# An order table redrawn, work for the tensor engine in early waits, and routing cut into pieces

## The chip, the core and the metric

The kernel runs on one core of a Trainium2 chip. The core has a tensor engine (TensorE, PE in the profile; its weight loads are shown apart as PEld), a vector engine (VectorE, DVE), a scalar engine (ScalarE, ACT), a general engine (GpSimd, POOL) and SyncE (SP), which here only issues transfers. Each runs its own queue in order; they meet at semaphores. The metric is device time in microseconds (us), and the time before is the median of three runs.

## What is computed

Attention first: for each of 8 batches and 8 heads, 512 tokens read from 32 states and the states read from the tokens. Both results together are 4,352 rows of 512 numbers. Then a mixture of 8 experts with soft routing: gate logits, a matrix P balanced by eight rounds of row and column normalization, and every expert applied to every row, weighted by P.

```
scores  = scale * x @ state.T          # softmax over states -> a
xread   = a @ state
scores2 = scale * state @ x.T          # softmax over tokens -> a2
sread   = a2 @ x
x = concat([xread, sread]) as (N, 512), N = 8 * (512 + 32)
P = exp(x @ w_gate - max)
for _ in range(8):
    P /= P.sum(1) + 1e-9
    P /= P.sum(0) + 1e-9;  P *= N / E
out = sum over e of P[:, e] * (relu(x @ w1[e]) @ w2[e])
```

(The reference here computes on N = 4,608 rows in the expert part's own set-up, but the kernel's rows are the 4,352 that attention gives.)

## The kernel before

Rows are handled in nine blocks: eight of 512 token rows (one per batch) and one of 256 state rows. The kernel has two stages.

The first stage does the attention, expert 0, the routing and the start of expert 1. It is a list of small operations (`op`), each with the engines it may run on, and `PLAN` is a table in the file that gives the order and the engine of each: `435P` is operation 435 on TensorE, V is VectorE, A ScalarE, G GpSimd, S a transfer from SyncE, H a step on the host side that only allocates. `issue` walks through the table and emits each operation; so the table sets the order of every engine's queue. An eviction (a copy out of PSUM) can be on ScalarE or on VectorE, as the table says.

Attention works in 16 units, two per batch (pairs of heads). For one unit: `turnX` (L578, by TensorE, batches 0 and 1) or a transposing transfer (L591, from SyncE, batches 2 to 7) turns x into `xT`; `score` (L605) makes scores in PSUM; the token side goes `flip` (L628), `maxA` (L631), `subA` (L648), `expA` (L656), `sumA` (L666), `normA` (L670), `flipA` (L674) and gives `aT`; the state side goes `maxB` (L640), `biasB` (L644), `expB` (L652), `recB` (L659), `normB` (L662), a transposing transfer to `ETs` (L742), and `read` (L758) with `keepS` into `xsT`. The first two units make the token side by matmul (`scoreA` L684, `turnA` L709) without the flips. Loads of x (L468) and of the weights w1 and w2 (L545, L548) are issued from GpSimd's queue; x has four buffers.

Expert 0 does not use the token rows themselves: w1 is projected through the states into V (L870), the hidden layer is V times `aT` (L897, eight per block), and the second product with w2 comes in half rows (L935, two halves for each 128 rows). The gate works likewise through a small product G (L520). The table mixes all this with attention, and then with the routing (part K, L814 to L846): a maximum, an exponential, and eight rounds of `rownorm` on VectorE (five instructions), a column sum by TensorE (L846) and `colnorm` (three instructions).

The second stage runs experts 1 to 7 in an order written out by hand: `layer1` makes the hidden layer of the next block (L255) while `layer2` does the seven Strassen-like products of this one (L334) and accumulates into `acc` (L348). Two PSUM banks (`seeds`) hold a running product; each was opened by a matmul with the identity (L353), and they are also used by `project` (L235), the projection for later blocks. `weigh` multiplies expert 0's result by its column of P (L296). `layer2_last` does the last block of the last expert: two rows of 128, and the transfers of the state rows to the output (L317).

Of the kernel before, what the change touches and what calls it, by code (L numbers as in the profile page):

```python
# [9 lines left out]
FP32 = mybir.dt.float32  # L10
# [7 lines left out]
46V 62P 50H 51G 61A 71V 63P 60A 52G 64V 11G 72V 73A 80P 65V 12G 435P 401P 66A 81V 13H 79P 14G 82V 436A 88V  # L18
437A 404P 83A 67V 402A 137H 403A 89V 96H 97P 100P 84V 406A 68V 90A 98A 15G 85V 69P 86P 53G 405A 99V 87V 70A
103P 101A 102A 91V 409P 16H 92G 413P 104V 407P 410A 411P 105V 111A 438P 120P 414V 408A 419P 421P 106V 415P  # L20
112V 138S 121V 74V 439A 412A 422V 113V 417P 107A 54G 440A 75G 122V 432P 429P 123V 370V 420A 469P 128A 418A
416A 17G 108V 140P 124A 125V 423P 426P 471A 433P 114A 148V 93S 129V 430P 149V 172H 424P 76S 434A 115V 470A
109G 130V 139S 110V 126G 141V 131A 427P 18G 127V 142V 428V 431A 445P 143V 132V 94P 150A 95V 77P 425A 156P 116G
447P 151V 133V 78V 449P 446A 443P 441P 144A 455P 164V 152G 448A 117S 19H 450V 157V 444A 165V 173S 442A 451P
456A 166A 134S 20G 452A 453P 463P 158V 472P 207H 145V 175P 159V 183V 184V 457P 31G 146G 454A 176V 473A 160A
464P 185A 174S 460P 458P 461P 465A 147V 161V 21G 153S 177V 191P 47P 162G 474A 118P 167V 459A 154P 462A 178V
163V 135P 49A 168G 199V 22H 48V 179A 466P 136A 352P 475P 200V 192V 201A 193V 119V 467P 476A 194V 23G 195A 485P
202V 208S 210P 180V 169S 155A 218V 356P 353A 481P 357V 468A 487P 219V 24G 489P 181G 186V 211V 242H 486A 482A
477P 490V 488A 483P 479P 220A 170P 478A 503P 187G 480A 484V 171A 203G 196V 537P 209S 25H 212V 226P 197G 504A
505A 506P 213V 500P 182V 198V 26G 234V 221V 507A 222V 204S 188S 491P 27G 538A 227V 539A 501P 497P 502A 508A  # L30
492P 235V 243S 228V 244S 214A 229V 511P 215V 236A 523P 230A 498P 494P 216G 245P 495P 515P 512V 499A 277H 231V
524A 493A 517P 246V 253V 223S 496A 247V 521P 516A 237V 254V 519P 509P 522V 518A 248V 513P 232G 189P 520A 255A
205P 510V 224P 514V 540P 28H 278S 261P 249A 190V 269V 29G 225A 270V 262V 531P 534P 206V 238G 250V 532P 256V
358P 271A 535P 217V 541A 533A 233V 542A 312H 279S 263V 272V 536A 354P 280P 528P 543P 529P 525P 288V 289V 251G
555P 264V 281V 265A 282V 239S 257V 526P 359A 266V 544A 530V 556A 545P 355A 547P 549P 273G 553P 527A 546V 571P
313S 290A 548A 283V 605P 550A 554V 296P 267G 606V 304V 572A 305V 240P 573A 557P 284A 607A 558A 551P 297V 552A
568P 360P 258S 241V 285V 30G 291V 306A 559P 562P 574P 298V 252V 315P 299V 286V 569P 576A 268V 323V 563P 575A
274S 300A 560P 570A 292G 316V 361A 561A 581P 564A 307V 565P 362P 324V 317V 301V 325A 302G 566P 363V 582A 326V
579P 587P 583P 287V 314S 588V 591P 567A 580A 639P 608P 584A 592A 347H 303V 331P 577P 348G 641V 640A 610A 609A
339V 293S 589P 585P 275P 332V 259P 578A 327G 586A 260A 590A 294P 340V 308G 333V 341A 593P 309S 318V 319A 334V  # L40
295V 364P 594P 276V 328S 625P 619P 342V 595A 335A 365A 599P 320V 602P 343V 336V 600P 337V 603P 626A 321G 322V
329P 310P 350G 344S 601A 349G 311A 620V 345P 338V 346V 604V 366P 596P 330A 368P 369V 351G 597P 367A 371V 611P
372P 598A 695H 615P 617P 373V 612V 374P 375V 613P 614V 616A 623P 618A 621P 696H 711H 376A 705P 377V 642P 624A
622A 706A 707A 630P 643V 697V 708P 644A 378P 379V 631P 710A 627P 698V 380V 647P 632A 709A 636P 628P 381P 633P
699V 648V 637P 382V 634P 657P 629A 638A 383V 700V 653P 658A 655P 384P 651P 635A 701V 654A 725P 385V 723P 386V
702V 656A 726A 716P 652A 724A 717A 645P 659P 649P 714P 646A 650A 660A 387P 721P 715A 712P 727P 687P 722A 388V
728A 688A 667P 713A 664P 389V 390P 703V 665P 668P 391V 673P 674A 392V 661P 670P 669A 729V 393P 671P 394V 666A
662P 672A 677P 395V 718P 663A 678A 679P 675P 683P 719A 681P 720V 680A 676A 685P 396P 684A 682A 397V 686A 692P
704V 689P 693P 690P 730P 398V 694A 399P 733P 731V 691A 732A 735A 734A 400V
""".split()  # L50
ENGINES = {"P": "PE", "V": "DVE", "A": "ACT", "G": "POOL", "D": "DMA", "S": "SPQ", "H": "HOST"}
NT_ = 2
# [52 lines left out]
def issue(ops):  # L105
    for step in PLAN:
        op = ops[int(step[:-1])]
        assert all(d.end for d in op.after) and ENGINES[step[-1]] in op.on
        for slot in op.takes:
            slot.ring.taken.append(slot)  # L110
            slot.tile = slot.make()
        op.emit(ENGINES[step[-1]])
        op.end = True
    assert all(op.end for op in ops) and len(PLAN) == len(ops)
# [3 lines left out]
def kernel(  # L118
# [63 lines left out]
    outs = out.rearrange("(b s) d -> b s d", s=SB)[:, S:, :]  # L182
# [80 lines left out]
    def layer1(e, bi):  # L263
# [6 lines left out]
        for j in range(NJ):  # L270
            for i in range(2):
                fb = i * NJ + j
                hps = bank([128, S], FP32, "hps", "h")
# [25 lines left out]
    def layer2_last():  # L299
# [4 lines left out]
        nb = 128 // Ns  # L304
        for row in range(tn // 128):
# [10 lines left out]
            for i in range(nb):  # L316
                (nc.scalar if i % 2 else nc.sync).dma_start(  # L317
                    out=outs[row * nb + i], in_=acc[ds(i * Ns, Ns), k, :])

    def layer2(e, bi, n):  # L320
# [30 lines left out]
        def seed(i):  # L351
            bb = bank([128, 2, DH], FP32, "Bseed", "B%d" % i)
            nc.tensor.matmul(bb.rearrange("p c d -> p (c d)"), identh, aT[:, 0, 0], start=True, stop=True)  # L353
            seeds.append(bb)

        if not n:
            for k, eng in enumerate(("DVE", "ACT", "DVE", "POOL")):
                weigh(k, eng)
        product(A, h(0, 0), w2h[:, :NJ, :DH], True)
        if not n:  # L360
            seed(0)
        Bb = seeds[n % 2]
        nc.scalar.copy(out=Bb[:, :nk], in_=A[:, :nk])  # L363
        yield
        product(Eb, s(0), T[:, 0], True)
        if not n:
            seed(1)
# [199 lines left out]
    for b in range(B):  # L567
# [30 lines left out]
        for q in range(NQ):  # L598
# [62 lines left out]
            def normB(eng, E2=E2, rrec=rrec):  # L661
                engines[eng].tensor_scalar(out=E2.tile, in0=E2.tile, scalar1=rrec.tile, scalar2=None,  # L662
                                           op0=ALU.mult)
# [33 lines left out]
            else:  # L697
                m0 = op(r(2), {"DVE": (0.63, 0.72)}, flip, [o2], [eA], [ps])
                m1 = op(r(3), {"DVE": (0.59, 0.68)}, maxA, [m0], [mxA], [eA])
                s1 = op(r(4), {"DVE": (0.60, 0.80)}, subA, [m1], [], [eA, mxA])  # L700
# [22 lines left out]
            n2 = op(r(3), {"DVE": (0.10, 0.25)}, biasB, [m2], [nsB], [nmB])  # L723
# [5 lines left out]
            f2 = op(r(6), {"DVE": (0.16, 0.26)}, recB, [e2], [rrec], [rowsum])  # L729
            f2 = op(r(6), {"DVE": (0.35, 0.48), "POOL": (1.56, 1.70)} if POOLB else {"DVE": (0.35, 0.48)}, normB, [f2], [], [E2, rrec])  # L730
# [33 lines left out]
            def keepS(eng, b=b, q=q, su=su):  # L764
                copy(eng, xsT[:, ds(2 * q, 2), ds(b * Ns, Ns)], su.tile)
# [38 lines left out]
    def sk(on, emit, after, **how):  # L804
        return op(rank, on, lambda _: emit(), after, **how)
# [6 lines left out]
    op((30.0,), {"DVE": (0.2, 0.3)}, lambda _: nc.vector.memset(ones128, 1.0))  # L812
# [8 lines left out]
    c = sk({"PE": (0.18, 0.45)}, lambda: nc.tensor.matmul(gb.tile, ones128[0:1, :], sm_["gm"]), [c], takes=[gb])  # L821
# [4 lines left out]
    for it in range(8):  # L826
        def rownorm():
            rsum = tile_of("rsum", [128, NTB])
            nc.vector.reduce_sum(out=rsum, in_=Pmat, axis=AX_X)
            nc.vector.tensor_scalar(out=rsum, in0=rsum, scalar1=EPS, scalar2=None, op0=ALU.add)  # L830
            nc.vector.reciprocal(out=rsum, in_=rsum)
            nc.vector.tensor_mul(Pmat, Pmat, rsum.unsqueeze(2).broadcast_to((128, NTB, E)))
            nc.vector.reduce_sum(out=tile_of("cpart", [128, E]), in_=Pmat.transpose([0, 2, 1]), axis=AX_X)

        csb = psum([128, E], FP32, "csb_ps")

        def colnorm(csb=csb):
            crec = tile_of("crec", [128, E])
            nc.vector.tensor_scalar(out=crec, in0=csb.tile, scalar1=EPS, scalar2=None, op0=ALU.add)
            nc.vector.reciprocal(out=crec, in_=crec)  # L840
            nc.vector.scalar_tensor_tensor(out=Pmat, in0=crec.unsqueeze(1).broadcast_to((128, NTB, E)),
                                           scalar=float(N) / float(E), in1=Pmat,
                                           op0=ALU.mult, op1=ALU.mult)

        c = sk({"DVE": (2.10, 2.25)}, rownorm, [c])
        c = sk({"PE": (0.25, 0.60)}, lambda csb=csb: nc.tensor.matmul(csb.tile, ones128, sm_["cpart"]),  # L846
               [c], takes=[csb])
        c = sk({"DVE": (0.75, 0.90)}, colnorm, [c], uses=[csb])
# [193 lines left out]
    for i, (e, bi) in enumerate(work):  # L1042
# [11 lines left out]
        if i:  # L1054
            next(v, None)
# [54 lines left out]
```

## Time and profile before

| | us |
|---|---|
| median of three runs | 753.16 |
| runs | 753.22, 753.16, 752.12 |
| the profiled execution | 752.75 |
| its span | 751.0 |
| PE busy from 0 to 10, from 10 to 20 | 3.15, 7.86 |
| PE busy from 50 to 60, from 60 to 70 | 8.99, 9.55 |
| PE busy from 200 to 300 | 100.00 |
| GpSimd busy from 11 to 101 | 43.90 |

The profile is of one execution. Busy times are those of each engine; matmuls are pipelined and their ends are modelled, so a full TensorE in this table need not be one at its peak. The granted clock is the share of TensorE's full clock that its throttle gave. A chain of waits follows the work that ended last back from the end, at each step to what released it.

### The profile page before, as it was taken

Reading aid. Unit: us, or ns where it says so; the run is one execution under the profiler, and the core shown is the slowest. Engines: PE = TensorE matmul, PEld = TensorE weight load, DVE = VectorE, ACT = ScalarE, POOL = GpSimd, SP = SyncE. Lnnn points to the kernel's source line nnn. Section 1 sums busy time; section 2 is a strip of 40 time slices with the busy share of each in tenths; the row PEclk is TensorE's granted clock in tenths of the full one; section 3 lists DMA queues with packets and bytes.
Section 4 is the critical chain, followed back from the end, with each engine's and each line's share of the span. In section 5 each row is a group of like instructions: output and inputs, shape, how many; then the busy total and the mean of one; then the engine's idle time right before and its main releaser. Section 6 shows DMA issues by size and latency. Waiting matters only on the chain.

```text
span 751.0 us, 16151 instructions
## 1 busy us (share of the span) xinstructions
PE 736.0 (98%) x6517; PEld 502.2 (67%) x6517; DVE 617.0 (82%) x1529; ACT 517.7 (69%) x1014; POOL 70.8 (9%) x81
## 2 busy tenths in 40 slices
PE   5999999999999999999999999999999999999997
PEld 3444445666777777776776767776777767767776
DVE  5899989877888789788888788887897888887885
ACT  6876856799876766667666766667666676667662
POOL 4674410200010000100000000100001000000000
PEclk9899999999999999999999999999999999999999
DMA  9997560600033000700007000330007000002234
GB/s 179 140 134 131 82 99 1 109 6 1 1 61 53 2 1 2 113 1 2 1 2 112 2 1 1 58 57 1 1 2 112 2 1 2 1 31 94 103 113 141
DMA packets 51323, 36.71 MB, mean 49 GB/s; under 512 B 25392, under 2 KB 43824, under 8 KB 51248
## 3 DMA queue, kind: packets, MB, share of 16 engines
q0 software_dynamic: 22272, 20.97, 18.5%
q1 hardware_dynamic: 27744, 14.18, 7.6%
q8 instruction: 51, 0.84, 0.5%
q10 hardware_dynamic: 1232, 0.52, 0.3%
q14 instruction: 24, 0.20, 0.1%
HBM read 42.48 MB, written 8.91 MB: 68 GB/s over the span
## 4 chain that ended last, share of the span: by engine, by line
PE 92%; DVE 3%; DMA 1%; ACT 1%; POOL 1%; issue 0%; SPq 0%; POOLq 0%; DVEq 0%; ACTq 0%
PE hps L255 28%; PE Bseed L334 20%; PE A L334 14%; PE E L334 14%; PE yps L935 6%; PE hps L897 4%; PE v_ps L235 4%; DMA xT<-x_nat 1%; DMA x_nat<-in_x_dram 1%; PE y L312 0%; PE v_ps L870 0%; POOL a L670 0%; ACT Hm L275 0%; DVE acc L348 0%; POOL E L662 0%; PE su_ps L758 0%
## 5 line engine op out<-in xcount | busy, mean ns | idle before, releaser
L275 ACT ACTIVATE Hm<-hps 128x512 f16<-128x512 f32 (+1 forms) x496 | 265.8, 577 | 130.5 <-PE hps L255 128.1
L255 PE MATMUL hps<-aT,V 128*128 128x512 f16 x880 | 230.6, 379 | 0.0
L334 PEld LDWEIGHTS <-Hm 128*128 128x128 f16 x1888 | 181.6, 98 | 71.3 <-issue 15.9
L348 DVE SCALAR_TENSOR_TENSOR acc<-Bseed,Pmat,acc 128x256 f32<-128x256 f32 x354 | 155.0, 477 | 9.8 <-PE Bseed L334 6.9
L334 PEld LDWEIGHTS <-sm 128*128 128x128 f16 x1416 | 138.3, 98 | 34.5 <-issue 0.3
L334 PE MATMUL A<-w2h,Hm 128*128 128x256 f16 x944 | 123.7, 273 | 0.0
L334 PE MATMUL Bseed<-T,Hm 128*128 128x256 f16 x944 | 123.3, 273 | 0.0
L255 PEld LDWEIGHTS <-V 128*128 128x128 f16 x880 | 86.1, 98 | 50.8
L348 DVE SCALAR_TENSOR_TENSOR acc<-E,Pmat,acc 128x256 f32<-128x256 f32 x236 | 103.2, 476 | 13.8 <-PE E L334 13.5
L281 DVE TENSOR_TENSOR sm<-Hm 128x512 f16<-128x512 f16 (+1 forms) x122 | 50.1, 411 | 60.4 <-ACT Hm L275 60.2
L243 ACT CAST V<-v_ps 128x512 f16<-128x512 f32 x144 | 74.2, 612 | 0.0
L348 DVE SCALAR_TENSOR_TENSOR acc<-A,Pmat,acc 128x256 f32<-128x256 f32 x118 | 51.9, 479 | 17.9 <-PE A L334 17.6
L935 PE MATMUL yps<-w2h,hT 128*128 128x512 f16 x272 | 64.1, 379 | 0.1
L334 PE MATMUL E<-w2h,sm 128*128 128x256 f16 x472 | 61.7, 273 | 0.0
L334 PE MATMUL E<-T,sm 128*128 128x256 f16 x472 | 61.6, 273 | 0.0
L334 PE MATMUL Bseed<-T,sm 128*128 128x256 f16 x472 | 61.5, 272 | 0.0
L363 ACT COPY Bseed<-A 128x512 f32<-128x512 f32 (+1 forms) x62 | 34.1, 550 | 37.9 <-PE A L334 35.3
L282 DVE TENSOR_TENSOR Hm<-Hm 128x512 f16<-128x512 f16 (+1 forms) x122 | 50.3, 412 | 4.2
L284 DVE TENSOR_TENSOR sm<-Hm,sm 128x512 f16<-128x512 f16 (+1 forms) x122 | 50.2, 412 | 4.2
L283 DVE TENSOR_TENSOR sm<-sm,Hm 128x512 f16<-128x512 f16 (+1 forms) x122 | 49.4, 405 | 0.0
L194 POOL DMA_DIRECT2D w1h<-in_moe_w_dram x12 | 8.5, 714 | 396.9 <-PE hps L255 396.5
L935 PEld LDWEIGHTS <-hT 128*128 128x128 f16 x272 | 25.4, 99 | 28.9 <-issue 1.8
(127 smaller groups left out, 617.7 us busy)
## 6 DMA issues: line engine op xcount, KB each, us to landing
w1h<-in_moe_w_dram POOLq DMA_DIRECT2D x16, 512.0 KB, 7.0
w2h<-in_moe_w_dram POOLq DMA_DIRECT2D x16, 512.0 KB, 8.4
out_dram<-acc SPq DMA_DIRECT2D x32, 256.0 KB, 2.5
x_nat<-in_x_dram POOLq DMA_DIRECT2D x16, 256.0 KB, 5.6
st_st<-in_state_dram ACTq DMA_DIRECT2D x1, 256.0 KB, 4.9
st_st<-in_state_dram SPq DMA_DIRECT2D x1, 256.0 KB, 4.2
ETs<-E SPq DMA_TRANSPOSE x16, 4.3
out_dram<-acc SPq DMA_DIRECT2D x4, 64.0 KB, 1.8
```

The costliest lines, as they stand in the source:

```text
L235: nc.tensor.matmul(ps[q][ds(j * Ns, Ns), :], stT[ds(r, 64), bi, q, ds((j ^ q) * Ns, Ns)], w1h[ds(r, 64), 2 * q + j // 2, cols], tile_posit ...
L243: nc.scalar.copy(out=dst, in_=src)
L255: nc.tensor.matmul(out, lhs, rhs, start=(k == 0), stop=(k == len(terms) - 1))
L275: nc.scalar.activation(out=Hm[:, i, j, :tn], in_=hps[:, :tn], func=AF.Relu)
L281: nc.vector.tensor_add(s1, a21, a22)
L282: nc.vector.tensor_sub(a21, a11, a21)
L283: nc.vector.tensor_sub(s2, s1, a11)
L284: nc.vector.tensor_sub(s4, a12, s2)
L334: nc.tensor.matmul(dst[:, c], lhs(j, c), rhs[:, j], start=first and c == 0 and j == 0, stop=(j == NJ - 1), skip_group_check=True)
L348: nc.vector.scalar_tensor_tensor(out=dst, in0=src[:, c], scalar=p[:, k], in1=dst, op0=ALU.mult, op1=ALU.add)
L363: nc.scalar.copy(out=Bb[:, :nk], in_=A[:, :nk])
L935: nc.tensor.matmul(yps.tile, hT[fb].tile[:, ds(tk * 128, 128)], w2h[:, fb, :], start=(fb == 0), stop=(fb == NFB - 1))
```

## The change

- `PLAN` is redrawn: order and engines of the first stage are new. In the new table 12 of 14 `subA` run on GpSimd, and three of the eight weight differences of expert 1 (`sums_w`); VectorE has 22 evictions of hidden matmuls instead of 16 and 6 of the second product instead of 3. The product for G stands ahead of the first hidden matmul. The routing starts earlier among TensorE's operations.
- `IDLE` names six operations, and how many 128-column matmuls with the identity TensorE does before each, into the tile that the operation then writes: 50 before the first transposes of x, 3 before each `scoreA`, 14 before the second half of the first projection, 8 before the transposes of x for batch 1, and 5 before the first `turnA`.
- `normB` on GpSimd becomes a two-input multiply with a broadcast operand.
- `rownorm` and `colnorm` become eight operations a round, so that the table can put others between them; the instructions are the same.
- The seeding matmuls go. The first hidden matmul of the second stage is written into the first of the two banks, which `layer1` is lent, and the first `layer2` step is split so that this comes between. The first four `weigh` steps are reordered.
- State rows are kept in another order in `xsT`, so that a row of 128 goes out in one transfer; the second row of the last block goes out in two halves, each after its part of the accumulation.

```diff
-def issue(ops):
+def issue(ops, idle):
     for step in PLAN:
...
+        idle(op.takes[0].tile if op.takes else None, IDLE.get(int(step[:-1]), 0))
         op.emit(ENGINES[step[-1]])
+IDLE = {56: 50, 63: 3, 80: 3, 452: 14, 97: 8, 69: 5}
...
+    def idle(t, n):
+        if not n:
+            return
+        t = t.rearrange({2: "p a -> p a", 3: "p a b -> p (a b)", 4: "p a b c -> p (a b c)"}[len(t.shape)])[:, :128]
+        for _ in range(n):
+            if t.dtype == FP16:
+                nc.tensor.transpose(t, identh, identh)
+            else:
+                nc.tensor.matmul(t, identh, identh, start=True, stop=True, skip_group_check=True)
...
-                engines[eng].tensor_scalar(out=E2.tile, in0=E2.tile, scalar1=rrec.tile, scalar2=None,
-                                           op0=ALU.mult)
+                if eng == "POOL":
+                    nc.gpsimd.tensor_mul(E2.tile, E2.tile, rrec.tile.broadcast_to((128, S)))
+                else:
+                    nc.vector.tensor_scalar(out=E2.tile, in0=E2.tile, scalar1=rrec.tile, scalar2=None, op0=ALU.mult)
...
-                s1 = op(r(4), {"DVE": (0.60, 0.80)}, subA, [m1], [], [eA, mxA])
+                s1 = op(r(4), {"DVE": (0.60, 0.80), "POOL": (1.05, 1.20)}, subA, [m1], [], [eA, mxA])
...
-                copy(eng, xsT[:, ds(2 * q, 2), ds(b * Ns, Ns)], su.tile)
+                copy(eng, xsT.rearrange("p c (g n b) -> p c g n b", g=B // nb, b=nb)[:, ds(2 * q, 2), b // nb, :, b % nb], su.tile)
...
-        c = sk({"DVE": (2.10, 2.25)}, rownorm, [c])
+        for emit, us, tail in ((row_sums, 0.43, 0.03), (row_eps, 0.20, 0.03), (row_rec, 0.37, 0.03),
+                               (row_mul, 0.45, 0.03), (col_part, 0.62, 0.15)):
+            c = sk({"DVE": (us, us + tail)}, emit, [c])
         c = sk({"PE": (0.25, 0.60)}, lambda csb=csb: nc.tensor.matmul(csb.tile, ones128, sm_["cpart"]),
                [c], takes=[csb])
-        c = sk({"DVE": (0.75, 0.90)}, colnorm, [c], uses=[csb])
+        for emit, us, tail in ((col_eps, 0.17, 0.03), (col_rec, 0.21, 0.03), (col_mul, 0.45, 0.15)):
+            c = sk({"DVE": (us, us + tail)}, emit, [c], uses=[csb] if emit is col_eps else [])
...
-            for i in range(nb):
-                (nc.scalar if i % 2 else nc.sync).dma_start(
-                    out=outs[row * nb + i], in_=acc[ds(i * Ns, Ns), k, :])
+                (nc.scalar if c + 1 < parts else nc.sync).dma_start(
+                    out=outs[row, :, :, cols], in_=acc[:, k, cols])
...
-        def seed(i):
-            bb = bank([128, 2, DH], FP32, "Bseed", "B%d" % i)
-            nc.tensor.matmul(bb.rearrange("p c d -> p (c d)"), identh, aT[:, 0, 0], start=True, stop=True)
-            seeds.append(bb)
...
+        if not i:
+            seeds += [bank([128, 2, DH], FP32, "Bseed", "B%d" % k) for k in range(2)]
         l2 = layer2(e, bi, i)
-        l1 = layer1(*work[i + 1]) if i + 1 < len(work) and work[i + 1] not in hid else iter(())
+        l1 = iter(())
+        if i + 1 < len(work) and work[i + 1] not in hid:
+            l1 = layer1(*work[i + 1], None if i else seeds[0].rearrange("p c d -> p (c d)"))
+        if not i:
+            next(l2)
+            next(l1)
```

## The prediction

> **What bounds the kernel now.** I read the page's engine shares first, then clock and busy time by stretch, then the chain of waits and the timeline around each place where TensorE (PE) ran thin. The shares alone:
>
> ```profile
> PE 736.0 (98%) x6517; PEld 502.2 (67%) x6517; DVE 617.0 (82%) x1529; ACT 517.7 (69%) x1014; POOL 70.8 (9%) x81
> ```
>
> TensorE looks full, but the ends of matmuls are modelled, so I counted the work it holds instead. In the first stage (attention, expert 0, routing: 0 to 135 us) the order table issues, at full-clock starting distances read from the timeline (a 512-column matmul 0.216 us, so a group of the hidden layer 0.432, a half row of the second product 0.864), some 114.5 us of work. The stage's last routing matmul sits after 114.1 us of that work and starts at 134.48: 20.4 us lost. Doing the same subtraction at other starts shows where: 13.7 us are lost at the first hidden matmul (18.86), 15.8 at the first second-layer matmul (24.88), 16.5 at the score matmuls of unit 8 (47.27), 18.3 at unit 9 (52.82), 18.9 at unit 10 (60.80), 19.4 when routing begins (100.97), then 20.3 from the first column sum on (105.95). The later experts run full. So only the first 25 us, 47 to 61 us, the seam and the tail can give anything.
>
> Busy time and clock by stretch, in the early part (columns: stretch, its length, busy of PE, PEld, DVE, ACT, POOL, then granted clock, DMA share, GB/s):
>
> ```profile
> 9.00:12.40 3.40, 3.12 (x46) 2.35 (x52) 2.60 (x9) 1.93 (x4) 0.00 (x0) 1.00 1.24 205
> 12.40:15.90 3.50, 2.01 (x40) 0.86 (x24) 3.43 (x8) 3.46 (x8) 0.00 (x0) 1.00 1.43 195
> 15.90:19.30 3.40, 3.02 (x26) 1.84 (x27) 3.08 (x8) 3.40 (x9) 0.14 (x1) 0.51 1.37 202
> 19.30:22.70 3.40, 3.40 (x16) 0.97 (x22) 2.86 (x5) 2.15 (x4) 2.19 (x2) 0.50 1.24 179
> ```
>
> After a thin stretch the clock is halved from 15.9 to 22.7, just when dense work arrives. The chain shows the price and the first wait; the second wait is the chain at 48 to 61:
>
> ```profile
> 1.43 5.38 DMA x_nat<-in_x_dram
> ...
> 6.86 1.03 PE xT_ps L578 x8
> ...
> 18.86 3.57 PE hps L897 x8
> ...
> 23.05 1.83 PE hps L897 x8
> ```
>
> ```profile
> 48.72 2.98 POOL E L662 x2
> ...
> 53.75 1.21 SPq L742
> ...
> 55.02 5.74 DMA xT<-x_nat
> ```
>
> Eight matmuls took 3.57 us, the next eight 1.83. VectorE is the second engine to watch: 29.06 us busy of 30 between 30 and 60 us. And it does exclude GpSimd: here its subtraction took 1.17 us beside a median of 0.68, ending half a microsecond after GpSimd's multiply, and GpSimd's next one took 1.99 beside 1.56.
>
> ```profile
> 41.54 1.04 POOL L670 TENSOR_TENSOR a<-eA,rA 128x512 f16<-128x512 f32 x1 [1.59 <-DVE rA L667]
> 41.96 1.17 DVE L648 TENSOR_TENSOR eA<-eA,mxA 128x512 f32<-128x512 f32 x1
> 42.57 1.99 POOL L662 TENSOR_SCALAR E<-E,rrec 128x512 f16<-128x512 f16 x1
> ```
>
> **The change, part by part.**
>
> *Fill, 83 matmuls.* Fifty stand before the first transposes, whose data land at 6.86. The identity they need is ready at 1.3, and 50 x 0.107 us (the cold distance: 8 transposes in 0.86 us) is 5.35, so they end near 6.7, inside the wait. That should warm the clock before 6.86 and shorten transposes (1.03 to about 0.6) and the state turns; VectorE's first real copy, at 8.35, moves some 0.6 to 0.8 earlier. I book nothing for it: the new table gives VectorE two more PSUM copies of 0.42 (the second half of unit 2's turned x, and the first aT) before the first hidden matmul, so that still starts near 18.9. The other 33 fill (3+3+14+8+5) at 0.057 us are 1.9 us; 27 stand between the second scores and the aT turns, in a stretch with 1.5 us idle of 3.5. If they hold the clock, the first eight hidden matmuls fall from 3.57 to 8 x 0.216: **-1.84**. Far end 0, if the clock drops anyway. Where a fill meets ready work it delays it: **+0.3**, between 0 and 1.9. [...]
>
> *Work moved into the early wait.* The gate-weight product (64 small matmuls, 0.72 us at 42.56 with nothing to hide it) and one projection half now stand before the first hidden matmul. I take **-0.7**, ends 0 and -0.95.
>
> *A transfer that then comes too late.* Second-layer products start at 18.9 + 3.46 + 0.9 (scores, gate, projection) = 23.2 in place of 24.88, and the fourth of them needs the second half of w2, now by 25.8; before, the fifth did, at 28.7. That load was issued at 20.70, behind GpSimd's 1.57 us normalization, and took 6.5 to land. With that step at 1.05 it lands at 26.7: **+0.8**, ends 0 and +2.
>
> *GpSimd's share.* Twelve subtractions (0.75 us each on VectorE) go to GpSimd; no row has them there, the nearest is its multiply of the same shape, 1.05. Its eleven normalizations become two-input multiplies: nearest rows 1.05 (two inputs, float32) and 1.56 (as now); I take 1.05. GpSimd's sum is 12 x 1.05 + 11 x 1.05 - 12 x 1.56 = +5.4 us on 43.9 busy of 90; VectorE is rid of 9 us, and gets back some fourteen evictions of 0.67. So the stall at 47 to 61, 2.4 us, hangs on whether the GpSimd, SyncE and DMA chain runs earlier. SyncE's transposes keep their order around unit 10 (those of E for units 6 and 7, then x), and TensorE asks for unit 10 after 39.7 us of its work instead of 41.9. Two normalizations 0.5 shorter each, less one subtraction 1.05 that joins the queue: about even. I take **-0.6**, ends -2.4 and +2.
>
> [...]
>
> *Routing in eight pieces.* The same instructions, one by one, so evictions slip between. It starts after 74.4 us of TensorE's work instead of 81.5, and its ten matmuls stand 3.6 to 5.8 us of work apart, before 3.7 to 5.0. A round of routing needs about 3.6 (3.1 on VectorE, 0.4 on TensorE), so cover is there; the 0.9 us lost at its start should shrink: **-0.2**, ends -0.9 and +1.5 (a round that lacks cover costs 0.5, three of them). The three weight differences on GpSimd lie beside it.
>
> *Seam.* Two seeding matmuls of 0.216 go (the first is issued between two products at 136.03): **-0.43**. The lent bank puts one relu of 0.60 ahead of the copy that the second product waits for; the other product, 0.87, covers it. Far end +0.5.
>
> *Tail.* The last accumulation ends at 747.50. Then each queue had two 64 KB transfers, issues of 0.58 each, 1.8 to 2.0 to land; now one of 128 KB, between 1.8 (64 KB) and 2.5 (256 KB): one issue less, slightly longer to land, **-0.45**, ends -0.6 and +0.2. The interleaved columns of xsT turn 16 copies of 0.2 us into strided ones; they lie beside TensorE's work.
>
> Sum: -1.84 + 0.3 - 0.7 + 0.8 - 0.6 - 0.2 - 0.43 - 0.45 = -3.1 against the profiled execution's 752.75 (span 751.0 and 1.75 around it). The median shown is 753.16, 0.41 above that execution, so **750.0**.
>
> **Rivals.** *Eaten downstream.* VectorE and DMA (share near 1 up to 60 us) pace the attention; TensorE only arrives earlier at the same waits. For it: VectorE's 29.06 of 30. Against: VectorE is rid of 9 us there, even if evictions take most of it. Left are seam and tail, -0.9: 752.3.
>
> *The clock falls again.* The fills add 1.5 us of TensorE work to a stretch that had 2.0 busy; where the threshold lies no row says. -3.1 + 1.84 and the load's wait of 0.8 gone with it: about 751.1, or 752 if the fill also delays.
>
> *Slower: GpSimd's queue holds up the x loads.* Loads of x are issued from the same queue, now behind subtractions that wait for VectorE's maximum, and exclusion lengthens both (1.17, 1.99). Each late x delays its turn on SyncE and a score on TensorE; waits of units 9 and 10 cost 2.4 already. Five batches load behind such steps; 1 us late each is +5, against the early -3.1: 755.0. It decides from 0.6 us a batch. For it: TensorE now asks for scores 13 to 15 2 to 6.5 us of work earlier. Against: GpSimd was idle for half of the time from 11 to 101.
>
> *Better.* The chain at 48 to 61 is cleared whole and the load isn't late: -1.8 for the chain and -0.8 for the load on top of -3.1: 747.4.
>
> **How the numbers follow.** Forecast 0.50, eaten 0.16, clock 0.10, slower 0.18, better 0.06. A measurement can tell 0.2%, 1.5 us, from no change: faster is below 751.65, slower above 754.67. Forecast, better and most of the clock rival are faster, with 0.64; the eaten case and the rest are the same, 0.17; 0.19 slower. The range goes from 747.0, short of the best end, to 755.0, the slower rival's middle; the forecast's own is 748.6 to 751.6.
>
> **What would show it.** Right: clock 1.00 from 16 to 23; eight first hidden matmuls in 1.8 us; second-layer start near 23.2; routing's last matmul about 2.3 us earlier than 134.48. Wrong: a wait of TensorE on w2 above 1 us, on xT at more units than 9 and 10, column sums that TensorE waits for, or subtractions on GpSimd at well above 1.05.

## The result, and the profile after

| | before | after |
|---|---|---|
| median (22 runs each) | 753.12 us | 755.46 us |
| lowest to highest | 751.48 to 755.81 | 753.23 to 761.09 |
| ratio, 95% interval | | 1.0037 (1.0025 to 1.0049) |
| profiled execution | 752.75 | 756.15 |
| its span | 751.0 | 754.4 |

The change makes the kernel slower by 2.3 us, where 3.1 us of gain was forecast. The two profiled executions, from which what follows is read, lie 3.4 us apart. The shares of the page hardly tell anything (TensorE has 81 matmuls more, VectorE 5.4 us less, GpSimd 7.3 more):

```profile
PE 739.9 (98%) x6598; PEld 507.5 (67%) x6598; DVE 611.6 (81%) x1526; ACT 513.6 (68%) x1003; POOL 78.1 (10%) x95
```

The early stretches of the changed kernel, with the columns as before (stretch, its length, busy of PE, PEld, DVE, ACT, POOL, granted clock, DMA share, GB/s). The last line is new: before, TensorE was busy 10.00 of 10 there, at clock 1.00.

```profile
9.00:12.40 3.40, 2.52 (x54) 1.68 (x55) 3.29 (x8) 2.45 (x6) 0.00 (x0) 1.00 1.26 210
12.40:15.90 3.50, 1.92 (x34) 1.45 (x31) 3.43 (x9) 3.17 (x7) 0.00 (x0) 1.00 1.42 192
15.90:19.30 3.40, 3.40 (x109) 2.45 (x107) 3.01 (x10) 3.23 (x8) 1.01 (x2) 1.00 1.37 202
19.30:22.70 3.40, 3.40 (x37) 1.51 (x35) 3.40 (x9) 3.20 (x8) 2.84 (x4) 1.00 1.29 139
30.00:40.00 10.00, 6.19 (x55) 2.41 (x53) 4.35 (x10) 3.94 (x10) 3.83 (x4) 0.68 1.24 161
```

So the fill did what it was for: the clock is 1.00 from 16 to 22.7, where it was 0.51 and 0.50. It held narrowly: from 12.40 to 15.90 TensorE was busy for 1.92 us, no more than before (2.01), and with the same fill on the old table the clock still fell for 3.4 us, from 16.39 in one run and from 14.81 in another (e1 and e4 below). In the nine traces of the new table with this fill it did not fall before 26 us; in the one without (e8) it fell at 14.67.

The kernel before also has 1.00 in the line from 9.00 to 12.40, but its trace holds no record of the clock before 12.53, where it rises; in the changed kernel it rises at 6.22. Eight transposes took 1.06 us at 9.39 before and take 0.62 at 8.11 now. So the kernel before worked at half clock up to 12.5 as well, which the prediction's reading of that column leaves out.

The loss lies from 30 to 40. The timeline of TensorE there, with the idle time ahead of a group and what ended it in brackets:

```profile
23.77 2.76 PE L952 MATMUL yps<-w2h,hT 128*128 128x512 f16 x12
27.08 3.61 PE L952 MATMUL yps<-w2h,hT 128*128 128x512 f16 x16 [0.55 <-DMA w2h<-in_moe_w_dram]
30.62 0.68 PE L761 MATMUL su_ps<-ETs,x_nat 128*64 128x32 f16 x32
35.11 0.41 PE L606 MATMUL psB<-xT,stT 64*32 64x256 f16 x8 [3.81 <-DMA xT<-x_nat]
35.46 1.89 PE L952 MATMUL yps<-w2h,hT 128*128 128x512 f16 x4
37.14 4.78 PE L914 MATMUL hps<-aT,V 128*128 128x512 f16 x14
```

The second-layer products start at 23.77 (24.72 before by the same view; the chain's start, which the prediction used, is 24.88). Then the scores of unit 5 wait 3.81 us for the transposing transfer of x, and the matmuls behind it are slow: four take 1.89 us where the clock-1.00 distance of 0.216 makes 0.86, fourteen take 4.78 instead of 3.02. The clock says why, in slices that begin and end where it changes or can change (same columns; the last section is about these steps of 3.41 us):

```profile
30.12:33.53 3.41, 1.18 (x35) 0.66 (x33) 0.95 (x2) 1.83 (x4) 2.69 (x3) 1.00 1.62 120
33.53:36.94 3.41, 1.83 (x12) 0.70 (x13) 1.34 (x3) 0.00 (x0) 0.00 (x0) 0.50 0.97 153
36.94:40.35 3.41, 3.41 (x9) 1.18 (x8) 2.29 (x6) 2.46 (x6) 1.04 (x1) 0.50 1.06 214
```

Where the late transfer comes from, the chain of waits shows (start, length, what):

```profile
24.40 0.28 SPq L745
...
24.73 10.34 DMA xT<-x_nat
...
35.11 0.41 PE psB L606 x7
35.53 1.82 PE yps L952 x4
37.35 4.57 PE hps L914 x14
```

The transfer is issued 2.1 us earlier than before (24.73; 26.83 before), and takes 10.3 us to land instead of 4.3. Right ahead of it GpSimd now issues both loads of x for batch 3 back to back, while the second half of w2 (512 KB, issued at 19.28, 7.8 us to land) is still in flight. GpSimd's queue, the changed kernel's:

```profile
22.77 1.05 POOL L649 TENSOR_TENSOR eA<-eA,mxA 128x512 f32<-128x512 f32 x1 [0.61 <-DVE nsB L645]
23.75 1.55 POOL L469 DMA_DIRECT2D x_nat<-in_x_dram  x2
25.66 1.04 POOL L673 TENSOR_TENSOR a<-eA,rA 128x512 f16<-128x512 f32 x1 [0.35 <-DVE rrec L660]
```

and the kernel's before, where the two loads are 4.2 us apart:

```profile
25.53 0.79 POOL L468 DMA_DIRECT2D x_nat<-in_x_dram  x1
...
29.74 0.81 POOL L468 DMA_DIRECT2D x_nat<-in_x_dram  x1
```

The twelve subtractions on GpSimd take 1.05 us in the mean and its eleven normalizations in the two-input form 1.04, as forecast. (The multiply in these lines is the token side's, which took 1.07 before too.)

The prediction's count of lost time (start of a matmul less the full-clock work in the table ahead of it) shows the course of the whole:

| start of | lost before | lost after | difference |
|---|---|---|---|
| second-layer products | 15.6 | 13.5 | -2.1 |
| scores of unit 5, then of unit 6 | | 18.2, 20.9 | |
| scores of unit 8 | 16.5 | 21.1 | +4.6 |
| scores of unit 9 | 18.3 | 22.2 | +3.9 |
| scores of unit 10 | 18.9 | 22.3 | +3.4 |
| routing | 19.4 | 23.7 | +4.3 |
| last column sum | 20.4 | 24.3 | +3.9 |

(The prediction has 15.8 in the first line, with the chain's start.) 2.1 us are gained up to 24 us, and 6.7 lost between there and unit 8. Of the 7.6 us that the changed kernel loses in that stretch, 0.55 is w2, 3.81 the wait for x, and 2.4 the halved clock (6.39 us for 18 matmuls in the chain, less 3.99 for the same 18 with the clock held, in an experiment below); 0.8 is spread over the rest.

### The profile page after: what moved, and what is told of

Its sections match the earlier page's. It is cut to its first block, busy times and chain, and to the rows that moved or that the text cites. A ratio compares the mean times of both kernels' runs of the same rounds, so it can differ in the third digit from the quotient of the medians.

```text
span 754.4 us, 16306 instructions
## 1 busy us (share of the span) xinstructions
PE 739.9 (98%) x6598; PEld 507.5 (67%) x6598; DVE 611.6 (81%) x1526; ACT 513.6 (68%) x1003; POOL 78.1 (10%) x95
## 3 DMA queue, kind: packets, MB, share of 16 engines
q0 software_dynamic: 22272, 20.97, 18.2%
## 4 chain that ended last, share of the span: by engine, by line
PE 91%; DMA 4%; DVE 2%; ACT 1%; POOL 0%; issue 0%; SPq 0%; POOLq 0%; ACTq 0%
PE hps L260 28%; PE Bseed L340 20%; PE A L340 14%; PE E L340 13%; PE yps L952 6%; PE v_ps L240 4%; PE hps L914 4%; DMA w1h<-in_moe_w_dram 1%; DMA xT<-x_nat 1%; DMA ETs<-E 1%; ACT hT L426 1%; PE v_ps L887 0%; PE su_ps L761 0%; PE y L319 0%; DVE acc L354 0%; ACT Hm L283 0%
```

## The experiments

Differences are medians against the kernel before in the same session; intervals are of the ratio.

**The fill alone, on the old table** (e1_fill_alone)

```diff
+IDLE = {56: 50, 63: 3, 80: 3, 404: 14, 97: 8, 69: 5}
-def issue(ops):
+def issue(ops, idle):
...
+        idle(op.takes[0].tile if op.takes else None, IDLE.get(int(step[:-1]), 0))
```

> The kernel before with the 83 fill matmuls alone, at the same six places. Theory (the fill works, the new table loses): the clock stays at 1.00 from 16 to 23 us, the first eight hidden matmuls take 1.8 us, and the time falls by 1.5 to 2.5 us, to about 751. Rival (VectorE and the transfers pace what follows, so TensorE only comes earlier to the same waits): within 0.7 us of before.

Measured: 753.25 against 752.81, ratio 1.0005 (0.9996 to 1.0013). The second-layer products start at 23.70 instead of 24.88, with the clock at 0.75 from 16 to 22.7. The gain of 1.2 us is then gone again. TensorE's waits between 14 and 70 us (line, what it waited for: us in total, times, longest):

```profile
PE v_ps L872 <- DMA w1h<-in_moe_w_dram: 1.4, 1, 1.4
PE su_ps L760 <- DMA ETs<-E: 1.3, 1, 1.3
...
PE psB L607 <- DMA xT<-x_nat: 0.7, 2, 0.4
```

Before, no wait for ETs stood in this list; now there is one of 1.3 us. On the old table the prediction's rival "eaten downstream" holds for the fill.

**Everything but the table** (e4_old_table): the changed kernel with the order and the engines of the table before; fill, the two-input form, seam and tail stay. The first place where the two tables part:

```diff
-... 12G 483P 449P 66A 81V 13H 14G 15G 53G 16H 82V 67V ...
+... 12G 483P 449P 66A 81V 13H 79P 14G 82V 484A 88V ...
```

> The changed kernel with the table of before (each routing bundle written out as its pieces in place, the weight differences mapped to their new numbers): fill, two-input normalization, seam and tail stay. Theory (only the new table loses): the gain of the fill and 0.5 for seam and tail, so 750 to 751. Rival (another part, as the two-input normalization on GpSimd or the pieces, loses): 753 or more.

Measured: 752.77 against 752.81, ratio 0.9999 (0.9990 to 1.0008). On the old table the other parts together neither cost nor gain; the loss of 2.3 us comes with the new table.

**One load of x moved back** (e2_x3_apart): the changed kernel with the second load of batch 3 (18G) behind GpSimd's next multiply (109G).

```diff
-... 17G 114A 464A 18G 477P 148V 108V 130V 109G 124A 139S ...
+... 17G 114A 464A 477P 148V 108V 130V 109G 18G 124A 139S ...
```

> The changed kernel with one step moved: the second load of x for batch 3 is issued after GpSimd's first normalization of the token side (unit 2) instead of right behind the first load. Theory (two loads back to back hold up the transposing transfer for unit 5): that transfer lands in about 5 us instead of 10.3, TensorE's wait before the scores of unit 5 falls from 3.8 to under 1 us, the clock isn't halved at 34 to 41, and the time falls by 4 to 6 us, to 750 or 751. Rival (GpSimd's longer queue and the exclusion hold up the attention as a whole): the wait moves or stays, and the time stays within 1 us of the changed kernel's 755.5.

Measured: 751.28 against 752.81, ratio 0.9974 (0.9963 to 0.9985); the whole change stood at +2.3, so this one step is worth some 3.9 us, and the kernel is faster than before. The load is issued at 26.80 instead of right behind its neighbour, and the chain reads:

```profile
24.72 7.68 DMA xT<-x_nat
...
32.74 0.97 PE yps L951 x4
33.71 3.02 PE hps L913 x14
...
43.56 6.22 DMA ETs<-E
```

The same transfer takes 7.7 us instead of 10.3, the wait is 1.59 instead of 3.81, and the 18 matmuls behind it take 3.99 us instead of 6.39, since the clock stays at 1.00. Part of it is given back at 49.92, where the state reads wait 1.73 us for ETs. (This profiled execution took 753.42, 2.1 above its kernel's median.)

**The clock held through the wait** (e3_fill_s5): the changed kernel with 70 more fill matmuls ahead of unit 5's scores.

```diff
-IDLE = {56: 50, 63: 3, 80: 3, 452: 14, 97: 8, 69: 5}
+IDLE = {56: 50, 63: 3, 80: 3, 452: 14, 97: 8, 69: 5, 156: 70}
```

> The changed kernel with 70 more fill matmuls (4.0 us at 0.057) ahead of the scores of unit 5, where TensorE waits 3.8 us. Theory (the wait costs twice, once itself and once by the halved clock after it): the wait for the transfer stays, the clock is 1.00 throughout, the 14 hidden matmuls behind it fall from 4.8 to about 3.1 us, and the time falls by about 3 us, to 752.5. Rival (VectorE and ScalarE pace what follows the wait, the clock does not matter): within 0.7 us of the changed kernel.

Measured: 757.70 against 752.81, ratio 1.0066 (1.0054 to 1.0078): slower than without. The clock is 1.00 from 30 to 40, and unit 8's scores start at 50.80 instead of 52.85, so 2.05 us are won there. Then unit 9 waits 2.73 for its x. The TensorE line, and the chain's piece that ends in it:

```profile
56.77 0.41 PE L606 MATMUL psB<-xT,stT 64*32 64x256 f16 x8 [2.73 <-DMA xT<-x_nat]
```

```profile
47.98 8.74 DMA xT<-x_nat
```

That transfer, too, is issued right behind two loads of x back to back (at 47.19), and the clock falls to 0.83 from 50 to 60 after the wait. The halved clock is a real part of the loss, but holding it only brings TensorE earlier to the next late transfer.

**The two loads put together in the kernel before** (e7_old_x3_pair)

```diff
-... 418A 416A 17G 108V ... 109G 130V 139S 110V 126G 141V 131A 427P 18G ...
+... 418A 416A 17G 18G 108V ... 109G 130V 139S 110V 126G 141V 131A 427P ...
```

> The kernel before with the suspected cost put in alone: the second load of x for batch 3 right behind the first. Theory: the transposing transfer for unit 5 lands in 6 to 9 us instead of 4.3; it was issued at 26.8 and is asked for at 33.3, so up to 2.5 us of wait and, if the clock drops, 1 to 2 more: 0.5 to 3 us slower than before. Rival (back-to-back loads are harmless, the new table's other order makes the transfer slow): landing 4 to 5 us, no change.

Measured: 754.40 against 752.70, ratio 1.0014 (1.0001 to 1.0026). Four of its eleven times lie from 751.9 to 752.4 and seven from 753.9 to 756.3, so the median's 1.7 us is more than the ratio's 1.1, and on the time the cost is only just shown. In the trace it is plain. The chain shows the transfer for unit 5 at 8.2 us instead of 4.3, with its issue hardly moved:

```profile
27.03 8.15 DMA xT<-x_nat
```

Unit 5 waits 1.72 us at 35.32, where it had not waited. The clock holds. So two loads together make that wait without anything else of the change.

**Both loads later; loads of batch 5 apart too** (e5_x3_later, e6_x3_x5_apart), from the changed kernel:

```diff
-... 17G 114A 464A 18G 477P 148V 108V 130V 109G 124A ...
+... 114A 464A 477P 148V 108V 130V 109G 17G 18G 124A ...
```

> The changed kernel with both loads of x for batch 3 issued after GpSimd's normalization of unit 2, so behind the transposing transfer for unit 5. Theory (what stands ahead of that transfer in the DMA engines decides its 10.3 us, of which one load apart left 7.7): it lands in 4 to 6 us, no wait of TensorE before the scores of unit 5, and the time is 1 to 2 us below the 751.3 of the run with the second load alone apart. Rival (weights, E transposes and x transposes alone fill the DMA engines there): landing stays near 7.7, time 751 or more.

```diff
-... 17G 114A 464A 18G 477P 148V 108V 130V 109G 124A ... 551P 23G 202V 218V 219V 534A 24G 170P 154P 181G ... 203G 213G ...
+... 17G 114A 464A 477P 148V 108V 130V 109G 18G 124A ... 551P 202V 218V 219V 534A 170P 154P 181G 23G ... 203G 24G 213G ...
```

> The changed kernel with the second load of batch 3 moved as before, and the two loads of batch 5 moved as well: one behind the normalization of unit 6 on the token side, one behind that of unit 7 on the state side. Theory (the wait just moves on: with unit 5 early, the E transposes for units 4 and 5 come behind two back-to-back loads of batch 5 and cost 1.7 us, and the clock drops at 50 to 55): that wait falls under 0.5 us, the clock stays at 1.00, and the time is 1 to 3 us below 751.3. Rival (the later loads make x late for units 10 and 11): a wait on xT of 1 us or more appears there, 751 to 753.

Measured: 753.64 against 752.70 (1.0015, 1.0007 to 1.0024) and 752.62 against 752.70 (1.0002, 0.9983 to 1.0021). With both loads behind it, unit 5's transfer lands in 4.7 us and nobody waits for it; but the loads are 3.2 us later, and so is batch 3: unit 6 waits 2.78 us for x at 38.10, and the reads 2.68 for ETs at 52.31. With batch 5 apart as well, unit 5 waits 0.20 and unit 9 not at all, but ETs is waited for 1.60 at 56.90. In e5 what is won at the transposing transfer is lost at the loads' own users, in e6 at the transfers of E.

Over these kernels, the time to land of unit 5's transfer goes with the loads of x issued just ahead of it. The columns are apart because w2's second half lands at about the time of the transfer's issue in before and e7 (0.4 us behind it and 0.5 ahead), and 1.9 to 2.7 us behind it in the others:

| loads of x within 2 us ahead | old table | new table |
|---|---|---|
| none | | e5: 4.7 us |
| one | before: 4.3 | e6: 7.1, e2: 7.7 |
| two | e7: 8.2 | after: 10.3 |

A second load adds 2.6 to 3.8 us. The 2 to 3 us from column to column are for the most part not w2's: in e4, on the old table with one load ahead and w2 in flight for 2.6 us more, the transfer took 5.1 us. Where they come from stays open. Nor must it be loads of x: in e9 and e10 below, where the transfer goes out at 19.04 and 19.18 right behind the 512 KB of w2, with no load of x just ahead, it took 10.4 and 9.0 us. In the traces of the kernel before and of the changed one, all 34 transfers issued from 17 to 48 us landed in the order of their issue, from whichever queue they came.

**That order without the fill** (e8_apart_no_fill): the kernel with one load moved back, and no fill.

```diff
-IDLE = {56: 50, 63: 3, 80: 3, 452: 14, 97: 8, 69: 5}
+IDLE = {}
```

> The changed kernel with the second load of batch 3 apart and without any fill matmul. Theory (the fill gives TensorE some 2 us at the start, but the transfer for unit 5 comes when it comes, and takes them back): within 1 us of the 751.3 with fill, the wait before unit 5 shorter. Rival (with the transfer mended the fill's 2 us show): 753 or more.

Measured: 755.26 against 752.70, ratio 1.0038 (1.0022 to 1.0055), 4.1 us above the same order with fill. Clock 0.59 from 16 to 22.7, and unit 9 waits 2.96 for x. The fill is worth nothing on the old table (e1), and 4 us on this one.

**Unit 5's transfer issued earlier** (e9_t5_early; e10_t5_early_x3_apart has in addition the move of e2):

```diff
-... 113V 138S 517P ... 109G 124A 139S 519A ...
+... 113V 138S 139S 517P ... 109G 124A 519A ...
```

> The changed kernel with one step moved on SyncE: the transposing transfer of x for unit 5 is issued right behind that for unit 4, ahead of the E transposes of units 0 and 1; both loads of batch 3 stay back to back. Theory (that one transfer's landing at 35.1 costs the change its gain): issued near 20 in place of 24.7, landed by 28, no wait of TensorE before unit 5, and the time falls by 3 to 5 us, to 751 or 752. Rival (the DMA engines are full from 20 to 40 and whichever transfer comes last is late): TensorE waits as long for the E transposes of units 0 and 1 or for units 6 and 7, and the time stays within 1.5 us of 755.5.

> Both moves together: the transfer for unit 5 early, the second load of batch 3 apart. Theory: the early part has no wait left, TensorE 1 to 2 us ahead of the run with the load alone apart at unit 6, and the time 750 to 751 if the later waits at units 4, 5 (states) and 9 don't grow. Rival (the DMA path paces the attention, and being earlier only lengthens the next wait): 751.3 or more.

Measured: 752.99 against 753.00 (0.9993, 0.9967 to 1.0019) and 752.06 against 753.00 (0.9983, 0.9966 to 1.0000); by the differences to before, e9 is some 2.3 us below the changed kernel, with this one step moved. Nobody waits at unit 5 any more, but in e9 the second half of w2 comes late:

```profile
29.26 5.23 PE L951 MATMUL yps<-w2h,hT 128*128 128x512 f16 x16 [2.54 <-DMA w2h<-in_moe_w_dram]
```

and its twelve times spread from 748.6 to 758.1. In e10 no wait is above 1.40 (w2, at 27.48), the clock is 1.00 from 10 to 70, and the profiled execution took 751.62; but the median is not below e2's.

**The second half of w2 early as well** (e12_w2_early), from e10:

```diff
-... 15G 53G 16H 82V ... 120P 54G 468A ...
+... 15G 53G 54G 16H 82V ... 120P 468A ...
```

> The kernel with unit 5's transposing transfer early and the second load of x of batch 3 moved back (752.06 as measured), with one more move: the load of the second half of w2 stands ahead of unit 1's state normalization on GpSimd's queue, so it is issued some 1.2 us earlier. Theory (the transfers between 15 and 60 us are one shared path, and a wait that is taken away comes back at the next transfer): the wait for w2 at 27.5 falls from 1.40 to under 0.4, but the waits for xT and ETs behind it grow by as much, and the time stays within 751.3 to 752.8. Rival (that wait was a loss of its own, only a matter of one issue standing too late): the time falls by the 1.4, to 750.2 to 751.0, and first score to routing start is shorter by about as much. A time above 753 would say that the earlier load holds up the first transfers of E or of x.

Measured: 753.63 against 753.17, ratio 1.0010 (0.9996 to 1.0025). Neither theory's window holds, but the case named last does. The move was much larger than stated there: with nothing else queued on GpSimd, the load goes out at 8.86 instead of 19.01. The wait for w2 is gone, but the last of the first loads of x land 0.7 us later than in e10, and unit 4's transfer 3.3. The chain:

```profile
6.05 12.37 DMA x_nat<-in_x_dram
18.44 7.86 DMA xT<-x_nat
```

Unit 4 waits 3.09 us at 26.34, and the clock halves behind it.

**The subtractions back on VectorE** (e11_sub_on_v), in the changed kernel:

```diff
-... 106G ... 123G ... 143G ... 159G ... 178G ... 194G ... 213G ... 229G ... 248G ... 283G ... 299G ... 318G ...
+... 106V ... 123V ... 143V ... 159V ... 178V ... 194V ... 213V ... 229V ... 248V ... 283V ... 299V ... 318V ...
```

> The changed kernel with its twelve subtractions back on VectorE at the same places of the table. Theory (GpSimd's share is not at fault, VectorE needs the relief): 9 us more on VectorE, attention later, 757 or more. Rival (GpSimd's longer queue and the exclusion hold up the loads of x): loads come earlier, 754 or less.

Measured: 768.09 against 753.00, ratio 1.0201 (1.0182 to 1.0221), 12.8 us above the changed kernel by the differences to before (15.1 and 2.3). From 70 to 100 us TensorE is busy 23.15 of 30, against 29.62 in the changed kernel. GpSimd's share is not what costs; this table needs it. (The table was made for GpSimd; what a table made for VectorE would reach was not tried.)

## Why the prediction was wrong

*Fill, -1.84 forecast.* Right, though narrowly, as e1 and e4 show. The clock rises at 6.22 (forecast: before 6.86) and is 1.00 from 16 to 22.7, and six of the first hidden matmuls take 1.40. First transposes 0.62 instead of 1.03, starting at 6.76; the first hidden matmul starts at 18.37, half a microsecond before the forecast's 18.9. The sum up to the second-layer products, -1.84 + 0.3 - 0.7 = -2.24, measured -2.1 in lost time.

*A transfer that then comes too late, +0.8 forecast.* This step failed. It named the second half of w2, and there it was right (0.55). But it asked this of one transfer only, and only from TensorE's side: which transfer is asked for earlier. The transposing transfer of x for unit 5 was asked for earlier too, and it also takes longer to land, because the table puts two loads of x right ahead of it. That is 3.81 us of wait, and 2.4 more of halved clock behind it: 6.2 us, none of it in the sum. A wait on xT at another unit than 9 and 10 is what the prediction itself had named as a sign of being wrong. That the clock halved behind the wait, and for how long, was in part chance, by the author's estimate (last section; mean clocks from 0.991 to 1.00 in 22 executions). e2 gets most of it back with one load moved; e7 makes the wait in the old kernel. The table of lost time shows the rest of the forecast running its course around it.

*GpSimd's share, -0.6 forecast.* The durations were right (1.05 each). VectorE's subtraction had taken 1.17 instead of 0.68 where it overlapped GpSimd's multiply, at 41.96 and 52.22 before; in the changed kernel none of GpSimd's subtractions, normalizations and multiplies took more than 1.08, whatever VectorE did beside them. The stall of 47 to 61 did shrink: 1.2 us lost from unit 8 to unit 10 instead of 2.4. But the kernel came there 4.6 us later, which gives the transfers time, so the runs do not show which of the two did it. From unit 10 to routing 1.4 us are lost (0.5 before), with one visible wait of 0.37 for ETs at 85.61; the rest was not followed up.

*Routing, -0.2.* Measured 23.7 to 24.3, 0.6 lost, instead of 19.4 to 20.4, 1.0: -0.4. *Seam, -0.43.* Not shown to be the seam's: from the first product of the second stage to the last group of outputs it took 607.94 us instead of 608.21, -0.27, but 608.32 with the same seam behind the old table (e4). *Tail, -0.45.* Mis-sized: 3.38 from the last accumulation to the end instead of 3.46, -0.08. The last output lands 2.12 us after that accumulation instead of 2.45; the issues of 64 KB, priced at 0.58 each, had taken 0.31 to 0.43. But from that landing to the end it takes 1.26 instead of 1.01: SyncE ends the program with a list of waits, gone through one after another every 0.06 us, and behind the one that the last transfer ends now stand six instead of two.

*The rivals.* "Slower: GpSimd's queue holds up the x loads" gave 755.0, near the measured 755.46, for the opposite reason. The loads of batch 3 were not held up: they went out earlier (23.75 and 24.56 instead of 25.53 and 29.74) and together. Later loads did go out later, the second of batch 4 at 42.75 instead of 39.13, but behind the wait of unit 5. e11 speaks against its cause as well, since with GpSimd relieved of the subtractions the time is far worse. "Eaten downstream" (752.3) is what e1 and e4 show on the old table. "The clock falls again" did not happen where it was put, but it did at 33.53, in a wait, where the prediction did not look. The threshold that it takes for granted no run shows: the clock held behind a window with TensorE busy for 0.50 of it and fell behind one with 0.55 (last section).

What the experiments settle: the loss comes with the table, not with the other parts (e4); its largest piece is the order of two loads and one transposing transfer (e2, e9, and e7 for the wait alone). What they do not give is an order without a late transfer. The waits go from unit 5 to units 4, 6 or 9, to ETs or to w2, and of the nine kernels made from the changed one e2 is the only one whose interval lies below the kernel before: 751.28 us, 0.9974 (0.9963 to 0.9985), from seven executions. That it is better than e10 (0.9966 to 1.0000) is not shown.

## What to carry to other kernels

When a change brings an engine to its work earlier, list every transfer that it needs in the next stretch, with when each is issued, what is issued just ahead of it on any queue, and when it would land; the one that the last version waited for least can be the next to wait for. Two loads that go out together can be dearer than the same two a few microseconds apart, not for their own users but for the transfer issued right behind them (8.2 us to land in e7 instead of 4.3 before). A wait of two to four microseconds also has to be priced with the slower clock that can follow it: the clock was halved behind 3.81 us in the changed kernel and 1.73 in e2, and not behind 2.78 and 2.68 in e5, so not each time, but with a chance, by where the wait lay on steps of 3.41 us.

## What the runs showed of the hardware

- The same transposing transfer of x took 4.3 to 10.3 us to land in the kernels of the table above, 3.8 more with a second load of x ahead of it on the old table and 2.6 to 3.2 more on the new; the two loads of batch 3 (256 KB each) took 4.2 to 4.7 before and 6.4 and 8.4 together in the changed kernel. One load of x had no other transfer in flight beside it, that at 42.75 in the changed kernel (DMA share 0.00 from 41.8 to 42.7 and from 47.1 to 48.7): it took 4.25 us from issue to landing, and none took under 4.2 in the traces of the two kernels.
- The clock's fall does not go by the length of the gap alone. In e2 it fell behind a gap of 1.73 us; in e5 it held through gaps of 2.78 and 2.68.
- In these runs the clock changed only on steps of 3.41 us. In each of the 14 traces the times at which it changes lie whole numbers of 3.41 us apart: 12.53, 15.94 and 22.77 in the kernel before (1 and 2 steps), 6.22, 33.53 and 40.35 in the changed kernel (8 and 2), 6.72, 51.09 and 54.50 in e2 (13 and 1). Where the steps lie differs from trace to trace. Busy time and clock, step by step around the gap in e2, and then for the two gaps in e5:

```profile
47.67:51.09 3.42, 1.69 (x52) 1.06 (x52) 1.94 (x6) 1.94 (x6) 2.46 (x3) 1.00 1.34 174
51.09:54.50 3.41, 3.41 (x31) 0.91 (x29) 2.71 (x6) 2.98 (x8) 1.32 (x2) 0.50 0.78 148
```

```profile
33.55:36.96 3.41, 1.78 (x9) 0.59 (x6) 1.72 (x5) 2.24 (x6) 2.61 (x3) 1.00 1.05 157
36.96:40.37 3.41, 2.27 (x18) 1.09 (x19) 1.89 (x5) 0.53 (x2) 1.22 (x2) 1.00 1.06 124
47.20:50.61 3.41, 2.42 (x26) 0.82 (x23) 3.17 (x9) 2.74 (x7) 3.09 (x4) 1.00 1.25 143
50.61:54.03 3.42, 1.72 (x38) 1.12 (x38) 1.15 (x3) 1.26 (x4) 0.96 (x1) 1.00 0.84 127
```

  In e2 the whole gap (48.19 to 49.92) lies in one window between two steps, of which TensorE was busy for 1.69 us, and the clock was halved for the whole next one, though that was full of work. In e5 a step cuts each of the longer gaps in two (at 36.96 and at 50.61), so that no window was idle for more than half, and the clock held. It fell behind windows of which TensorE was busy for a share of 0.09 (e12, 23.19 to 26.60), 0.35 (the changed kernel, 30.12 to 33.53), 0.49 (e2) and 0.55 (the kernel before, 12.53 to 15.94), and held in windows of 0.50 and 0.52 (e5) and 0.57 (the changed kernel, 13.05 to 16.46). It held at 0.50 and fell at 0.55, so the busy share alone does not tell.
- The mean clock differs between executions of one kernel: of the 22 of the changed kernel the two with 1.00 took 753.23 and 753.24 us, the one with 0.991, the lowest, 761.09. That the same wait costs the halved clock in one execution and not in another is the author's estimate from this; no two traces of one kernel show it.
- In the profiled execution of the changed kernel the clock was at 0.50 from 33.53 to 40.35, for two windows, 5.2 us of it dense work; the wait for x ran on into the first of them, of which TensorE was busy for 1.83 us, and the clock came back only behind the second.
